# Causal attention and a gated FFN in one kernel: stores held back, two batches' DMA transposes split, and the order of the first three tiles placed anew

## The chip, the cores and the metric

One core of a Trainium2 chip. The metric is the time of one execution on the device, in microseconds (us). Each kernel is run several times, in rounds with the kernel before on the same chip. Differences below 2%: the class is "same".

## The reference

```python
q, k, v: (8, 8, 576, 64) float32            # batch, heads, sequence, head dim
w_gate, w_val: (512, 1536);  w_out: (1536, 512)

scores = q @ k.T / sqrt(64)
scores = where(block(i) >= block(j), scores, -1e9)   # blocks of 64 positions
attn   = softmax(scores) @ v
x      = attn.transpose(0, 2, 1, 3).reshape(4608, 512)
out    = (relu(x @ w_gate) * (x @ w_val)) @ w_out    # (4608, 512) float32
```

## The kernel before

The FFN works on nine tiles: tile j (0 to 7) is the first 512 positions of batch j, and the ninth is the last 64 positions (the "tail") of all eight batches. Attention of batch j + 1 is put between the FFN products of tile j. A table `AT` gives each piece of attention, load, cast or store a position, counted in FFN products (144 a tile), and a loop gives the pieces out in that order:

```python
for n in sorted(acts, key=lambda n: AT[n]):
    ffn(int(AT[n]) - place[0])                 # FFN products up to that position
    place[0] = max(place[0], int(AT[n]))
    acts[n]()                                  # then the piece itself
```

A position is only a place in the order of each engine's instructions. An engine that has nothing to wait for runs ahead of it.

The names in the table that this document needs:

```python
"q24":  # GpSimd casts q and k of batch 2, heads 4 to 7, from float32 staging to bf16 (2 x 128x1024);
        # SyncE transposes each by DMA into "perm" once it is cast
"v2":   # GpSimd casts v of batch 2 (2 x 128x1024)
"td0", "td1", "td2":  # VectorE casts half of the tail keys and of tail v of batch 0, 1, 2 (64x256 each)
"u0".."u3":  # copies from "perm" to qTm and kTm: q and k of batch 2, head pairs 0 to 3, by the engines
             # (q's, k's) named in HOW
"s8".."s15": # scores of round r = 4 * batch + head pair;  "x8".."x15": its output transposed to xT
"S0".."B2":  # the tails of batches 0 to 2; "A" and "B" are their two products with v
"d3":   # batch 3's q and k transposed by DMA: 2 main parts, 2 tails
```

Of the tiles that the traces name, xT is x transposed, the FFN's input; hT is relu(gate) times value, which VectorE writes for the FFN's second product; attnT is the exponential of the scores; qTm, kTm, qTt and kTt are q and k transposed, "mains" (the first 512 positions) and tails.

Batch 3's transposes go to SyncE's queue together, the tile's stores leave as each is done (those of tile 0 alone are held), and a tail's transpose follows at once on the tail's last product:

```python
def dma_transposes(b):
    m, tl = bfs[b, 0], bfs[b, 1]
    for t in range(2):
        nc.sync.dma_start_transpose(
            (qTm, kTm)[t][b % 2].rearrange("p c h n -> p (c h) n"), m[t])
    tails_by_dma(b, tl)                      # qTt, then kTt
...
# in the FFN, for each output group of tile j:
ob = sb.tile([128, 512], FP, name="ob", bufs=4)[:, 0 : n1 - n0]
nc.vector.tensor_copy(ob, op)
if store:
    store.pop()()
(store if j else late).append(lambda j=j: put(j, s, ob, n0, n1))   # put: DMA from ScalarE
...
# in a tail's piece:
def end():
    tail_av(b, 1, x)
    tail_to_xT(b, x)
```

(The code is cut.)

The softmax here doesn't subtract the row's maximum and nothing guards it: scores larger than these inputs give would overflow.

## Time and profile before

| | |
|---|---|
| median of 3 runs | 363.15 us (362.9 to 364.13) |
| the execution that was profiled | 365.12 us, span of the trace 363.3 |
| TensorE busy | 353.3 us of 363.3 (97%) |
| VectorE, ScalarE, GpSimd busy | 47%, 46%, 31% |
| TensorE idle 0 to 23, 95 to 116, end | 4.54, 1.81, 3.59 us |

A page of the profile lists each engine's busy time; the table of stretches gives it for chosen pieces of the span; the timeline shows single instructions with, in brackets, the idle time ahead of them and what ended it. A matmul's listed length runs past the start of the next, so waits of TensorE are counted here as start-to-start distance above what the same matmul takes when nothing is waited for (0.216 us for 512 columns, as the prediction works out). The execution in the trace took 2 us more than the median. The lines themselves are in the prediction below.

### The profile page before, as it was taken

How to read it: one execution, taken by the hardware profiler on the slowest of the kernel's cores; microseconds unless marked ns; L12 is line 12 of the kernel's file. 1: busy time of each engine (PE TensorE's matmuls, PEld its weight loads, DVE VectorE, ACT ScalarE, POOL GpSimd, SP SyncE). 2: the span in 40 equal slices, each digit the busy share in tenths (PEclk: the TensorE clock that was granted, in tenths of full speed). 3: DMA queues.
4: the chain of work that ended last, by engine and by line, in shares of the span. 5: the costliest groups of instructions: out<-in, count | busy, mean ns of one | idle time of the engine just before them, and what ended most of it. 6: DMA issues, size and time to landing. Idle time of an engine off the chain costs nothing.

```text
span 363.3 us, 7423 instructions
## 1 busy us (share of the span) xinstructions
PE 353.3 (97%) x2933; PEld 176.9 (49%) x2933; DVE 170.7 (47%) x426; ACT 167.9 (46%) x265; POOL 112.8 (31%) x157
## 2 busy tenths in 40 slices
PE   7899999999998999999999999999999999999996
PEld 3544455545544555555555454554455544444443
DVE  4663456677433363444445443554255434333432
ACT  4933676696325850666055625553365403302310
POOL 4647645695209500680049001930000000000000
PEclk9999999999999999999999999999999999999999
DMA  8999999999999995899449951997220130031013
GB/s 245 298 357 374 314 239 255 189 156 138 186 203 108 141 154 137 56 146 186 109 49 145 169 133 46 130 157 152 81 16 14 54 102 0 0 88 29 1 41 105
DMA packets 152083, 49.97 MB, mean 138 GB/s; under 512 B 134512, under 2 KB 145008, under 8 KB 152048
## 3 DMA queue, kind: packets, MB, share of 16 engines
q0 software_dynamic: 70480, 8.85, 46.7%
q1 hardware_dynamic: 76480, 31.86, 44.8%
q10 hardware_dynamic: 5088, 8.78, 7.2%
q8 instruction: 23, 0.38, 0.5%
q14 instruction: 12, 0.10, 0.1%
HBM read 37.75 MB, written 9.44 MB: 130 GB/s over the span
## 4 chain that ended last, share of the span: by engine, by line
PE 89%; DMA 5%; ACT 4%; DVE 1%; issue 0%; POOL 0%; SPq 0%; POOLq 0%; DVEq 0%
PE ffnp L663 49%; PE ffnp L748 23%; PE sc L450 3%; PE ffnp L585 2%; PE one L450 2%; DMA xT<-xnat 2%; DMA stage<-in_moe_w_gate_dram 2%; PE one L585 2%; ACT attnT L414 2%; PE one L663 1%; ACT attnT L455 1%; PE ffnp L547 1%; PE one L794 1%; DMA kTt<-k_bt 1%; PE ffnp L599 1%; PE one L599 1%
## 5 line engine op out<-in xcount | busy, mean ns | idle before, releaser
L679 DVE TENSOR_TENSOR hT<-gate_sb,ffnp 128x512 bf16<-128x512 bf16 x106 | 72.6, 685 | 96.5 <-PE ffnp L663 70.7
L673 ACT ACTIVATE gate_sb<-ffnp 128x512 bf16<-128x512 f32 x103 | 62.1, 605 | 103.3 <-PE ffnp L663 93.6
L663 PE MATMUL ffnp<-xT,wv 128*128 128x512 bf16 x376 | 100.7, 379 | 0.0
L663 PE MATMUL ffnp<-xT,wg 128*128 128x512 bf16 x364 | 99.0, 379 | 1.1 <-DMA xT<-xnat 0.4
L748 PE MATMUL ffnp<-wo,hT 128*128 128x512 bf16 (+2 forms) x444 | 98.8, 373 | 0.0
L748 PEld LDWEIGHTS <-hT 128*128 128x128 bf16 x444 | 41.8, 98 | 45.5 <-issue 0.6
L663 PEld LDWEIGHTS <-wv 128*128 128x128 bf16 x432 | 40.1, 98 | 45.5 <-issue 3.2
L663 PEld LDWEIGHTS <-wg 128*128 128x128 bf16 x432 | 39.8, 98 | 44.6 <-issue 3.6
L455 ACT ACTIVATE attnT<-sc 128x1024 bf16<-128x1024 f32 x56 | 56.8, 1044 | 0.0
L758 DVE COPY ob<-ffnp 128x512 f32<-128x512 f32 (+2 forms) x37 | 25.0, 676 | 45.1 <-PE ffnp L748 44.7
L338 POOL DMA_DIRECT2D q_bf<-in_q_dram x20 | 17.8, 903 | 76.3 <-DVE hT L679 52.0
L462 ACT ACTIVATE attnT<-one 128x512 bf16<-128x512 f32 (+1 forms) x28 | 15.0, 536 | 53.8 <-PE ffnp L450 53.8
L585 PEld LDWEIGHTS <-attnT 128*128 128x128 bf16 x640 | 26.5, 97 | 13.9 <-DVE attnT L803 1.3
L338 POOL DMA_DIRECT2D v_bf<-in_v_dram x30 | 24.3, 853 | 6.8 <-PE one L585 2.2
L450 PEld LDWEIGHTS <-kTm 64*128 64x128 bf16 x384 | 11.3, 94 | 15.6 <-issue 7.8
L338 POOL DMA_DIRECT2D k_bf<-in_k_dram x20 | 17.7, 933 | 0.0
L450 PE MATMUL sc<-qTm,kTm 64*128 64x512 bf16 (+1 forms) x168 | 16.9, 305 | 0.0
L585 PE MATMUL ffnp<-v_bf,attnT 128*128 128x65 bf16 x320 | 15.0, 194 | 0.0
L462 ACT ACTIVATE attnT<-ffnp 128x512 bf16<-128x512 f32 (+1 forms) x28 | 15.0, 534 | 0.0
L803 DVE MEMSET attnT<- 64x128 uint32 x59 | 9.0, 165 | 12.0 <-ACT attnT L455 10.2
L524 DVE TENSOR_TENSOR xnat<-ffnp,recip 128x256 bf16<-128x256 f32 x32 | 13.6, 424 | 1.1
L585 PE MATMUL one<-v_bf,attnT 128*128 128x65 bf16 x250 | 11.6, 193 | 0.7 <-POOL v_bf L220 0.7
(122 smaller groups left out, 293.8 us busy)
## 6 DMA issues: line engine op xcount, KB each, us to landing
out_dram<-ob ACTq DMA_DIRECT2D x29, 256.0 KB, 2.4
stage<-in_moe_w_val_dram SPq DMA_DIRECT2D x6, 512.0 KB, 8.2
stage<-in_moe_w_gate_dram SPq DMA_DIRECT2D x6, 512.0 KB, 8.7
stage<-in_moe_w_out_dram SPq DMA_DIRECT2D x6, 512.0 KB, 10.5
q_bf<-in_q_dram POOLq DMA_DIRECT2D x20, 128.0 KB, 4.3
k_bf<-in_k_dram POOLq DMA_DIRECT2D x20, 128.0 KB, 5.8
v_bf<-in_v_dram POOLq DMA_DIRECT2D x20, 128.0 KB, 6.1
stage<-in_v_dram SPq DMA_DIRECT2D x19, 128.0 KB, 5.4
```

Of the source, the lines that this page charges most:

```text
L338: ins = nc.gpsimd.dma_start(dst, part_of)
L450: nc.tensor.matmul(o, kTm[b % 2][head_of(hh), c, hp, :], qT, start=True, stop=True)
L455: return lambda: nc.scalar.activation(at[:, :, lo : lo + 512], sc, AF.Exp, scale=scale)
L462: nc.scalar.activation(at[:, hh, 1024 : 1024 + w], third[hh][:, 0:w], AF.Exp, scale=scale)
L524: nc.vector.tensor_tensor(out=out, in0=av[:, 0:m, 0:64], in1=recip[:, 0:m].to_broadcast([rows, m, 64]), op=AX.mult,)
L585: nc.tensor.matmul(av[:, p, :], at[:, col : col + 128], v_bf[b % 2][:, c, h, :], start=(p == 0), stop=(c == p), skip_group_check=True,)
L663: nc.tensor.matmul(to, (wg, wv)[t][f // 4][:, c, 128 * (f % 4) : 128 * (f % 4) + 128], x[:, c], start=(c == 0), stop=(c == 3),)
L673: nc.scalar.activation(gate_sb, gate, AF.Relu)
L679: nc.vector.tensor_tensor(out=h, in0=gate_sb, in1=val, op=AX.mult)
L748: nc.tensor.matmul(op, hT[f][:, 128 * s : 128 * (s + 1)], wo[f // 4][:, f % 4, n0:n1], start=(f == 0), stop=(f == 11),)
L758: nc.vector.tensor_copy(ob, op)
L803: nc.vector.memset(o, 0.0)
```

## The change

Its intent: take DMA work (tile 1's stores, the tails' transposes) out of the stretch around 95 to 116 us, where TensorE waits for DMA transposes; split batch 3's and batch 4's transposes into parts, and put batch 3's in another order and place; and place the order of everything in tiles 0 to 2 anew. The functional part:

```diff
-    def dma_transposes(b):
+    def dma_transposes(b, which=(0, 1, 2)):
         m, tl = bfs[b, 0], bfs[b, 1]
-        for t in range(2):
+        for t in which:
+            if t == 2:
+                tails_by_dma(b, tl)
+                continue
             nc.sync.dma_start_transpose(...)
-        tails_by_dma(b, tl)
...
-                xtails[b] = sb.tile([64, 512], BF, name="xtail", bufs=2)
+                xtails[b] = sb.tile([64, 512], BF, name="xtail", bufs=4)
...
-                (store if j else late).append(lambda j=j: put(j, s, ob, n0, n1))
+                (store if j > 1 else late).append(lambda j=j: put(j, s, ob, n0, n1))
...
             def end():
                 tail_av(b, 1, x)
-                tail_to_xT(b, x)
...
+                f"X{b}": lambda: tail_to_xT(b, x),
```

The table of positions has nearly 200 changed lines. Sorted by place (the start, positions below 140, is cut; its lines swap loads and casts of weights):

```diff
-            "td1": 164.5,
+            "td1": 155.98,
             "td0": 156.81,
...
-            "A0": 174.52,        # products with v of batch 0's tail
-            "B0": 178.89,
+            "A0": 180.62,
+            "B0": 184.99,
...
-            "u1": 190.06,
-            "u0": 190.06,
-            "v2": 191.07,
-            "q24": 191.07,
+            "q24": 190.06,
+            "u0": 190.39,
+            "u1": 190.39,
...
-            "u2": 207.72,
+            "v2": 203.58,
+            "u2": 203.99,
-            "s9": 208.6,
+            "s9": 206.14,
...
-            "d3": 260.7,
+            "d30": 263.9,        # q mains
+            "d32": 263.9,        # both tails
+            "d31": 263.91,       # k mains
-            "s12": 312.27,
+            "s12": 318.08,
...
+            "o4": 325.51,        # tile 1's stores
+            "X1": 330,           # tail of batch 1 to x
+            "X0": 332,
+            "o5": 339.19,
+            "o6": 352.67,
+            "X2": 355.13,
+            "o7": 366.92,
...
-            "u0": ("pool", "pool"),      # HOW: engines of the copies of q and k
-            "u1": ("dve", "dve"),
+            "u0": ("pool", "dve"),
+            "u1": ("pool", "dve"),
             "u2": ("dve", "dve"),
-            "r8": ("dve", "one", "ffn", None),
+            "r8": ("dve", "one", "ffn", ("dve", "sc")),   # x of round 8 over TensorE, not DMA
```

## The prediction

> **What bounds the kernel now.** I read the page's busy shares first, then the table of stretches, then the timeline of the one stretch in which TensorE is not full, and last the chain of waits. The first two lines are from the page, the rest is the table of stretches (busy us and instructions of each engine, granted clock, DMA share, GB/s).
>
> ```profile
> PE 353.3 (97%) x2933; PEld 176.9 (49%) x2933; DVE 170.7 (47%) x426; ACT 167.9 (46%) x265; POOL 112.8 (31%) x157
> ...
> DMA  8999999999999995899449951997220130031013
> ...
> 0.00:10.00 10.00, 7.26 (x42) 3.14 (x42) 4.50 (x14) 5.35 (x7) 5.01 (x21) 1.00 0.89 251
> 10.00:23.00 13.00, 11.20 (x147) 6.72 (x145) 9.05 (x27) 8.99 (x15) 6.89 (x13) 1.00 1.15 316
> 23.00:60.00 37.00, 37.00 (x291) 18.92 (x290) 18.03 (x42) 21.70 (x38) 22.56 (x27) 1.00 1.08 307
> 60.00:95.00 35.00, 34.90 (x395) 18.45 (x394) 23.99 (x63) 22.49 (x36) 22.86 (x29) 1.00 1.55 174
> 95.00:116.00 21.00, 19.19 (x170) 9.17 (x168) 7.17 (x16) 8.50 (x13) 6.31 (x8) 1.00 1.49 164
> 116.00:200.00 84.00, 84.00 (x774) 42.83 (x774) 40.33 (x113) 41.60 (x66) 34.81 (x45) 1.00 1.46 125
> 200.00:297.00 97.00, 97.00 (x827) 48.62 (x824) 44.70 (x120) 44.90 (x70) 14.35 (x18) 1.00 0.82 97
> 297.00:363.30 66.30, 62.71 (x303) 29.09 (x301) 22.89 (x34) 14.33 (x24) 0.00 (x0) 1.00 0.13 38
> ```
>
> TensorE sets the time. Of 363.3 us it is idle 10.05: 2.74 in the first 10 us, 1.80 up to 23 us, 0.10 from 60 to 95, 1.81 from 95 to 116, and 3.59 after its last matmul (eviction and store). From 116 to 297 it is not idle at all. No edit of this change can speed up those 181 us or the end, so all it can win lies in the 1.81 us in the middle and some of the 4.54 us of the start. The middle in the timeline, TensorE and the queue of SyncE:
>
> ```profile
> 97.34 5.46 SPq L347 DMA_TRANSPOSE qTm<-q_bf  x1
> ...
> 98.35 0.34 ACTq L647 DMA_DIRECT2D out_dram<-ob  x1
> ...
> 101.91 0.59 PE L663 MATMUL ffnp<-xT,wg 128*128 128x512 bf16 x2
> ...
> 102.77 0.38 PE L663 MATMUL ffnp<-xT,wg 128*128 128x512 bf16 x1 [0.26 <-DMA xT<-xnat]
> ...
> 103.03 3.81 SPq L347 DMA_TRANSPOSE kTm<-k_bf  x1
> 103.31 0.38 PE L663 MATMUL ffnp<-xT,wg 128*128 128x512 bf16 x1 [0.16 <-DMA xT<-xnat]
> ...
> 106.95 1.18 SPq L116 DMA_TRANSPOSE qTt<-q_bt  x1
> ...
> 107.58 1.03 PE L663 MATMUL ffnp<-xT,wv 128*128 128x512 bf16 x4
> ...
> 108.24 1.21 SPq L117 DMA_TRANSPOSE kTt<-k_bt  x1
> ...
> 109.00 0.28 PE L450 MATMUL one<-qTm,kTm 64*128 64x256 bf16 x1 [0.40 <-DMA kTm<-k_bf]
> ...
> 109.97 0.82 PE L663 MATMUL ffnp<-xT,wg 128*128 128x512 bf16 x3
> ...
> 111.76 0.29 PE L472 MATMUL one<-qTt,kTt 128*128 128x64 bf16 x4 [0.96 <-DMA kTt<-k_bt]
> ```
>
> Three waits, all for DMA transposes: tile 2's x (third and fourth product), batch 3's keys (its first scores), batch 3's tail keys. The chain of waits (start, length) goes through the same transposes:
>
> ```profile
> 95.97 7.30 DMA xT<-xnat
> ...
> 108.24 3.47 DMA kTt<-k_bt
> ...
> 328.60 20.72 PE ffnp L663 x96
> ```
>
> The last line is the rate: 20.72 / 96 = 0.2158 us a product. With it the waits have their true size, start to start: 102.77 - (101.91 + 2 x 0.216) = 0.43; 103.31 - 102.77 - 0.216 = 0.32; 109.00 - (107.58 + 4 x 0.216) = 0.56; 111.76 - (109.97 + 3 x 0.216) = 1.14. Sum 2.45 us, more than the 1.81 of idle time, since a matmul's shown length runs past the start of the next.
>
> **What the Trainium skill says.** "TensorE: Matmul & The Clock Gate", Step-by-step: what each phase is for, gives about 216 ns between 512-column products back to back; the trace has 215.8. "Perfetto Trace Analysis", Identifying the Most-Contended Engine, says that matmul busy time misjudges the distance to the roofline; the same product is listed at 379 ns, so I count starts. "DMA: Bandwidth & Descriptors", Issuing engines are not separate DMA queues, says that transfers of all issuers run on the same 16 engines and interleave. It agrees: the x transpose issued at 95.97, among GpSimd's loads and ScalarE's stores, took 7.30 us to land, where the tile's median is 3.9. "Perfetto Trace Analysis", DMA Instruction — HWDGE (DVE, Sync), says that the issuing instruction ends with the generation of descriptors, before the data has moved: keys took 3.81 us to issue and were still waited for at 109.00, 5.97 after the issue began.
>
> **The change, part by part.** Positions in the table of the schedule count FFN products, 144 a tile; tile 2 begins at 288, which TensorE reaches at 101.91.
>
> 1. Stores of tile 1. Their positions are 325 to 367 instead of right after each eviction. The stores at 98.35 and (in the timeline too) 93.97 and 102.81 leave the busy stretch. A store holds 256 KB, so 0.77 MB; at the 164 GB/s of this stretch that is 4.7 us of transfer, at the 316 of the start 2.4. There are four output buffers, and tile 2 needs the first again near 396, after all four stores: no wait. Nothing on TensorE.
>
> 2. Tails' transposes to x. Those of batches 0, 1 and 2 go to 332, 330 and 355. One (batch 1, formerly at 83.74) leaves the stretch before tile 2; 1.2 us of SyncE's queue. Four buffers instead of two make this legal. Read only in the last tile (328 us): no wait.
>
> 3. Round 8's x goes over TensorE instead of DMA: 4 transposes of 128 columns, about 4 x 0.056, and a change between chains of near 0.1: +0.33 us of TensorE. One DMA transpose less (1.2 us of issue); its DVE copy of 0.42 lies beside.
>
> 4. Batch 3's transposes. Equal positions keep the listing's order, so the order is: q mains, both tails, k mains. The tail keys' wait (1.14) should vanish. But the last x transpose comes later: its round's second product with v moves from 259.11 to 263.76, and the tail's scores of batch 2 (0.76 with their changes of array shape) now go ahead of it. Counting TensorE: 94.27 for round 10's second half, +0.31, +0.22, +0.76, +0.22, +0.31, +0.43 gives 96.5; DVE adds 1.15 as before, so x is issued near 97.65, not 95.97. Then q mains from 99.0 for 3.2 to 5.5 us (4.3), tails 2 x 1.24, k mains from 106.0. Landing takes 4.3 at the least, median 5.9: 110.3 to 111.9. If both issues are fast, 109.1.
>
> 5. Batch 3's scores move from 312.27 to 318.08 (+5.8 x 0.216 = 1.25). Without waits TensorE is there at 101.91 + 0.33 + 30 x 0.216 + 0.6 for a tail product = 109.3. So the wait for keys is not 0.56 but between 0 and 2.6; I take 1.3. The x waits (0.75) should go: 97.65 plus about 4 lands before 102.9, where the fourth product wants it.
>
> Middle: -2.45 - 0.15 (the scores' first pair, which lost time as well: 109.01 to 109.31 in the timeline for 256 columns that take 0.11) + 0.33 + 1.3 = about -1.0 us.
>
> 6. Start. The order of the q and v loads stays; the first gate and value weights swap, so gate weights land about 1.5 us earlier. In the timeline, though, TensorE's last wait of the start is for x of head pair 2, whose copy on ScalarE (20.33) stood behind the cast of the second gate weights, which waited 2.42 us for their load. That load keeps its place behind the same bytes. And a cast of value weights (about 0.6) is now put on ScalarE between the two: the copy may come at 20.9. Against that, pair 3's transposes now stand ahead of those products. I count +0.2, between -0.6 and +0.7.
>
> 7. Rounds 12 to 15 take other PSUM banks, tails of batch 2 and batch 4's q and k transposes other places. From 116 on there is no TensorE idle time to win; I count 0, at worst +0.5.
>
> Sum: -1.0 + 0.2 + 0 = -0.8: 363.15 - 0.8 = about 362.3. Because the new placing looks searched for, and my figures for queues are the pessimistic end, I say 362.2.
>
> **Rivals.** (a) Everything works: no wait at keys, none at x, 0.5 gained at the start: -2.6 + 0.33 - 0.5, about 360.4. For it: issue times of 2.8 for k mains occur when DMA is quiet. (b) The wait only changes its name: k mains are now last in SyncE's queue and wait 2.6 or more, perhaps slowed by batch 4's loads, which begin at 109.7 before; then the middle gains nothing, and with the start's +0.2 to +0.7 the time is 363.5 to 364. For it: the queue is in order, and q mains and tails before keys take 6.8 us of it. (c) The stretch is bound by GpSimd's small loads, not by stores: they hold 46.7% of the engines' time in the page's list of queues against 7.2% for stores. Then x still lands late, 0.5 us of wait stays, and 362.8 results. I think (a) 25%, (b) 30%, the rest between.
>
> **Range and chances.** Repeats of before spread from 362.9 to 364.13. From (a) and (b) I take 360.6 to 364.0. 2% is 7.3 us; the idle time within reach is at most 6.4, and a loss of 7 would need several new waits of the largest size seen. Faster 1%, same 98%, slower 1%.
>
> **What would show it.** Right: 116 to 297 stays full; no TensorE wait for kTt; the x waits are gone or under 0.3; the one wait left in the middle is for kTm at batch 3's first scores, 0.5 to 2.5 us; no store is issued between 90 and 110. Wrong: a wait for xT over 0.5 us; a new TensorE wait after 116; TensorE's start of dense work off from 22 us by more than 0.7; or kTm issued before 104 and not waited for, which would make it 360.5.

## The result, and the profile after

| | before | after |
|---|---|---|
| median | 363.02 us (4 runs, 362.79 to 364.13) | 364.08 us (4 runs, 363.84 to 364.63) |
| profiled execution, its span | 365.12 us, 363.3 | 364.63 us, 362.8 |

Ratio 1.0025, 95% interval 1.0001 to 1.0049: class same, and by about 1 us slower. A ratio here is the mean time of one kernel's fast runs over that of the other's of the same rounds, so it is not quite the ratio of the medians.

The table of stretches of the changed kernel (columns as in the prediction: stretch, length, then busy us and instructions of PE, PEld, DVE, ACT, POOL, the granted clock, DMA share, GB/s):

```profile
10.00:23.00 13.00, 10.87 (x145) 6.80 (x146) 9.41 (x29) 9.11 (x14) 5.19 (x11) 1.00 1.15 316
60.00:95.00 35.00, 33.31 (x360) 17.61 (x358) 24.55 (x56) 21.96 (x36) 24.38 (x29) 1.00 1.49 167
95.00:116.00 21.00, 21.00 (x216) 11.10 (x215) 9.62 (x24) 8.79 (x15) 5.06 (x7) 1.00 1.10 118
116.00:200.00 84.00, 84.00 (x775) 42.74 (x774) 39.78 (x111) 41.86 (x66) 36.55 (x49) 1.00 1.44 137
```

The middle, 95 to 116, is full: 21.00 of 21 instead of 19.19. Of the 1.81 us that were idle there, 1.59 have come back as idle time from 60 to 95: 33.31 busy instead of 34.90. The start lost 0.3 more than before (10.87 instead of 11.20).

The middle in the timeline, SyncE's queue and the first scores of batch 3:

```profile
101.22 1.96 SPq L350 DMA_TRANSPOSE qTm<-q_bf  x1
103.28 1.58 SPq L116 DMA_TRANSPOSE qTt<-q_bt  x1
104.96 1.21 SPq L117 DMA_TRANSPOSE kTt<-k_bt  x1
106.35 1.32 SPq L350 DMA_TRANSPOSE kTm<-k_bf  x1
...
111.22 0.28 PE L452 MATMUL one<-qTm,kTm 64*128 64x256 bf16 x1
```

The order is the one predicted: q mains, tails, k mains. The keys, issued at 106.35, landed at 110.62; TensorE asked for them at 111.22, so nothing waits. But TensorE is there 1.9 us later than the 109.3 that the prediction worked out. It lost most of them from 62 to 66 us:

```profile
61.87 1.04 POOL L195 CAST q_bf<-stage 128x1024 bf16<-128x1024 f32 x1 [0.87 <-DMA stage<-in_q_dram]
62.01 1.04 DVE L207 CAST k_bt<-stage 64x256 bf16<-64x256 f32 x1
...
63.22 1.05 POOL L195 CAST k_bf<-stage 128x1024 bf16<-128x1024 f32 x1 [0.32 <-DMA stage<-in_k_dram]
63.40 1.02 DVE L207 CAST k_bt<-stage 64x256 bf16<-64x256 f32 x1
...
64.56 0.38 PE L296 MATMUL ffnp<-ident,k_bt 128*128 128x128 bf16 x4 [0.64 <-DVE k_bt L207]
64.77 0.69 DVE L681 TENSOR_TENSOR hT<-gate_sb,ffnp 128x512 bf16<-128x512 bf16 x1
```

The same VectorE instructions in the kernel before:

```profile
61.58 0.29 DVE L207 CAST k_bt<-stage 64x256 bf16<-64x256 f32 x1
...
62.84 0.69 DVE L679 TENSOR_TENSOR hT<-gate_sb,ffnp 128x512 bf16<-128x512 bf16 x1 [0.65 <-PE sc L663]
...
64.51 0.29 DVE L207 CAST k_bt<-stage 64x256 bf16<-64x256 f32 x1
```

A 64x256 cast took 0.29 us and now takes 1.04 and 1.02, both times beside a GpSimd cast of 1.04 or 1.05 that began 0.14 to 0.18 us ahead of it and ended about 0.15 us before it. In the order of the change, GpSimd's casts (`q24`) come ahead of the copies `u0` and `u1`, and VectorE's tail casts of batch 1 (`td1`) directly ahead of those of batch 0 (`td0`); so two pairs of casts meet. VectorE takes its instructions in order: the product hT comes at 64.77 instead of 62.84, and TensorE waits 0.80 us at 63.73 for the tail keys and 0.77 at 65.31 for the bank (a piece of the memory that TensorE writes to) that hT frees. Further on it waits 0.61 at 76.34, also for hT, and 0.29 at 50.02, for a VectorE memset of attnT.

In the chain of waits the two products hT (64.77, 1.30 us) now stand, and the DMA transposes that stood there before (7.30 for xT and 3.47 for kTt) are gone.

### The profile page after: what moved, and what is told of

Read it like the earlier page. It is cut to its first block, busy times and chain, and to the rows that moved or that the text cites. A ratio compares the mean times of both kernels' runs of the same rounds, so it can differ in the third digit from the quotient of the medians.

```text
span 362.8 us, 7419 instructions
## 1 busy us (share of the span) xinstructions
PE 352.5 (97%) x2937; PEld 177.7 (49%) x2937; DVE 173.8 (48%) x426; ACT 167.6 (46%) x265; POOL 114.9 (32%) x158
## 4 chain that ended last, share of the span: by engine, by line
PE 91%; DMA 3%; DVE 2%; ACT 1%; POOL 1%; issue 1%; SPq 0%; DVEq 0%; POOLq 0%
PE ffnp L665 49%; PE ffnp L750 26%; PE sc L452 3%; PE ffnp L587 2%; PE one L452 2%; PE one L587 2%; DMA stage<-in_moe_w_gate_dram 2%; DMA stage<-in_k_dram 1%; PE one L665 1%; PE ffnp L549 1%; PE ffnp L601 1%; DVE hT L681 1%; PE one L601 1%; ACT attnT L416 1%; PE sc L587 1%
## 5 line engine op out<-in xcount | busy, mean ns | idle before, releaser
L338 POOL DMA_DIRECT2D k_bf<-in_k_dram x20 | 18.5, 960 | 0.0
L587 PE MATMUL ffnp<-v_bf,attnT 128*128 128x65 bf16 x300 | 14.0, 194 | 0.2
L526 DVE TENSOR_TENSOR xnat<-ffnp,recip 128x256 bf16<-128x256 f32 x30 | 12.7, 425 | 1.0
L665 PE MATMUL ffnp<-xTt,wg 128*128 128x512 bf16 x48 | 12.3, 379 | 0.0
```

The source lines that it names most:

```text
L338: ins = nc.gpsimd.dma_start(dst, part_of)
L526: nc.vector.tensor_tensor(out=out, in0=av[:, 0:m, 0:64], in1=recip[:, 0:m].to_broadcast([rows, m, 64]), op=AX.mult,)
L587: nc.tensor.matmul(av[:, p, :], at[:, col : col + 128], v_bf[b % 2][:, c, h, :], start=(p == 0), stop=(c == p), skip_group_check=True,)
L665: nc.tensor.matmul(to, (wg, wv)[t][f // 4][:, c, 128 * (f % 4) : 128 * (f % 4) + 128], x[:, c], start=(c == 0), stop=(c == 3),)
```

## The experiments

Twelve kernels in three groups of four; each group ran on one chip, five rounds, with the kernel before beside it. Before's own runs were in group 1: 364.85, 362.92, 362.81, 362.77, 362.58, 364.11, 362.43, 362.54, 367.11, 363.11, 362.66; in group 2: 362.4, 362.25, 362.53, 364.62, 364.77, 362.3, 362.64, 364.67, 362.59, 362.28, 362.83; in group 3: 363.27, 365.32, 362.55, 362.63, 362.43, 362.65, 364.22, 362.48, 364.93, 362.34, 364.84. So the kernel before has two levels, 362.25 to 363.27 (23 runs) and 364.11 to 367.11 (10 runs), with nothing between them, although none is 1.5% above the fastest and so none counts as slow. The granted clock does not tell them apart: 0.993 to 1.000 in the lower, 0.995 to 1.000 in the upper. Keep this in mind with every interval below: they are about ±0.4% wide, mostly because of this.

| kernel | median us | runs over 364 | ratio to before, 95% interval |
|---|---|---|---|
| before, again (1) | 364.53 | 4 of 6 | 1.0028 [0.9985, 1.0071] |
| after, again (1) | 365.23 | 6 of 6 | 1.0047 [1.0010, 1.0084] |
| early part old, late part new (1) | 363.16 | 0 of 6 | 0.9998 [0.9962, 1.0035] |
| early part new, late part old (1) | 364.57 | 6 of 6 | 1.0039 [1.0002, 1.0076] |
| after, GpSimd casts behind the copies (2) | 363.25 | 1 of 6 | 1.0009 [0.9980, 1.0038] |
| before, GpSimd casts ahead (2) | 362.67 | 0 of 6 | 0.9988 [0.9958, 1.0018] |
| before, tile 1's stores held (2) | 363.90 | 3 of 6 | 1.0015 [0.9983, 1.0047] |
| early old, late new, tail transposes behind (2) | 367.58 | 6 of 6 | 1.0123 [1.0088, 1.0158] |
| after, casts behind and copies' engines as before (3) | 363.69 | 3 of 6 | 1.0009 [0.9975, 1.0042] |
| early old, late new, stores at once (3) | 364.07 | 4 of 6 | 1.0023 [0.9988, 1.0058] |
| early old, late new, keys ahead of tails (3) | 362.66 | 0 of 6 | 0.9982 [0.9951, 1.0013] |
| after, one tail cast back (3) | 364.08 | 4 of 6 | 1.0013 [0.9981, 1.0045] |

My theory going in: the early part of the new order costs 1.5 to 2 us through the casts that meet, and the late part wins back what the middle had lost. The rivals: the late part itself costs (held stores come back as collisions later), or the gain in the middle was never there in an ordinary execution.

### 1. Both kernels again

No edit.

> The kernel before, unchanged, for a second trace of it. Both theories: ratio 1.000. The theory that the middle waits vary from run to run (the profiled run of before took 365.12 us, its timed runs 363.0): this trace has less than the 2.45 us of waits for the x, key and tail-key transposes between 95 and 116 us, near 0.5 to 1. The rival that the profile is typical: again 2.2 to 2.7 us there.

> The changed kernel, unchanged, for a second trace. Both theories: ratio 1.002 to 1.004 to before, 364.1 us; the waits at 63.7, 65.3 and 76.3 us (0.80, 0.77, 0.61 us start to start) come again within 0.2, since they come from the order of casts on VectorE and GpSimd and not from DMA; no TensorE wait between 95 and 116 us.

The second trace of the kernel before fell on an execution of 362.65 us (span 360.8):

```profile
60.00:95.00 35.00, 34.90 (x395) 18.45 (x394) 24.03 (x63) 22.50 (x36) 22.67 (x29) 1.00 1.61 182
95.00:116.00 21.00, 21.00 (x195) 10.60 (x192) 9.25 (x22) 8.99 (x14) 7.03 (x9) 1.00 1.35 157
```

There is no idle time in the middle (0.5 to 1 us of waits was expected). The three waits of 2.45 us that the whole prediction was about belong to the execution of 365.12 us, and 363.3 - 360.8 = 2.5 us is just their size. What differed is the DMA. Two stretches of 1 us of the trace before (first fence), and the first of them in the trace of the ordinary execution (second fence); the last column is GB/s:

```profile
86.00:87.00 1.00, 1.00 (x15) 0.57 (x14) 0.54 (x4) 1.00 (x2) 1.00 (x2) 1.00 1.86 24
87.00:88.00 1.00, 1.00 (x15) 0.64 (x14) 1.00 (x3) 0.28 (x1) 0.77 (x1) 1.00 0.26 21
```

```profile
86.00:87.00 1.00, 1.00 (x15) 0.54 (x14) 0.53 (x4) 1.00 (x2) 1.00 (x2) 1.00 1.27 92
```

In the execution of 365.12 us, 28 packets, nearly all of 128 or 256 bytes and each over 0.9 us long, were under way from 85.40 for 2.56 us, while a DMA transpose of x began (85.92) amid GpSimd's loads; in the ordinary one nine, from 85.13 for 1.46 us. After it, GpSimd's first load of v landed at 97.28 instead of 93.17, the last x at 103.27 instead of 101.47, kTm at 108.96 instead of 107.01 and kTt at 111.71 instead of 108.76. Such standstills (six or more packets of at most 512 bytes, each over 0.9 us long, overlapping) of 1 to 3 us are in every trace, six to eleven each; whether the upper level of the times is always such a longer standstill I can't show, since only one trace fell on each level.

The changed kernel had, again, 0.77 at 65.52, 0.61 at 76.54 and 0.29 at 50.92, and a new wait of 0.75 at 145.09 for tile 3's x. The wait of 0.80 for the tail keys did not come again, a miss of this expectation: GpSimd's first cast came later in this execution (63.76 instead of 61.87), both of VectorE's key casts took 0.29, and the cast that met it was the one of tail v behind them (1.07 us from 63.87), so that only hT was late. Which casts meet, and whether the loss is 1.57 or 0.77 us, varies between executions.

### 2. Which half of the new order costs

Edit: all positions under 200 and their engines of one kernel, the rest of the other.

> Positions and engines of all that lay before 200 as in the kernel before, the rest (held stores, held tail transposes, split batch-3 transposes, round 8 over TensorE) as changed. Theory 1, the early part loses 2 to 2.5 us and the late part gains 1 to 1.5: 361.6 us, ratio 0.996. Theory 2, the late part gains the whole 2.5 us of the profile and the early loses 3.5: 360.6. Theory 3, the late part is what costs and the early is harmless: 364 us.

> The reverse: the changed kernel's places and engines before 200, the kernel before from there on, stores of tile 1 and tail transposes at once. Theory 1: 365.2 us, ratio 1.006, with the waits of 63.7, 65.3 and 76.3 us and those of the middle both there. Theory 2: 366.5. Theory 3: 363.

Early new, late old has the changed kernel's waits again (0.92 at 63.70, 0.77 at 65.40, 0.61 at 76.43, 0.30 at 49.98) and 1.19 in the middle, and all its runs are at 364.25 or above. Early old, late new has none of them and stays between 362.48 and 363.94. So the loss is in the early part. The gain that the theory gave the late part did not come: early old, late new was to take 361.6 us, 0.996 of before, and takes 363.16, 0.9998. What is left in the middle of early old, late new is one wait for keys, 0.64 start to start:

```profile
103.33 1.32 SPq L350 DMA_TRANSPOSE kTm<-k_bf  x1
...
109.08 0.28 PE L452 MATMUL one<-qTm,kTm 64*128 64x256 bf16 x1 [0.48 <-DMA kTm<-k_bf]
```

This is the wait that the prediction put at 1.3, and which the changed kernel hides by coming late. The issue took 1.32 us, but the keys landed 5.70 after its start. The Trainium skill ("Perfetto Trace Analysis", DMA Instruction — HWDGE (DVE, Sync)) says that the profiler shows the issue without the movement of the data; the trace agrees.

### 3. Is it the casts?

```diff
 # after, GpSimd casts behind the copies
-            "q24": 190.06,
+            "q24": 190.5,
```

> The changed kernel with one position moved: GpSimd's casts of batch 2's second half (q24) from 190.06 to 190.5, behind the unpermuting copies, as the kernel before has them. Theory of the shared port (VectorE's tail casts wait for GpSimd's casts beside them: 1.04 and 1.02 us instead of 0.29): the casts take 0.29 again, TensorE's waits at 63.7 and 65.3 us (0.80 and 0.77 start to start) go, the one at 76.3 stays; 1.3 us less than the changed kernel, ratio to before 1.001. Rival, VectorE's queue (batch 1's tail cast was moved ahead, from 164.50 to 155.98, and fills VectorE at the wrong moment): casts 0.29, but at least 0.5 us of those waits stays.

VectorE's two key casts took 0.29 again (62.04 and 62.68), both waits near 64 and 65 us are gone, and the ratio is 1.0009 where the changed kernel's own had been 1.0025 and 1.0047 (the intervals overlap; the trace is the evidence). The wait of 0.6 near 75 stays. The Trainium skill ("SBUF — State Buffer", Who interferes with whom) says that VectorE and GpSimd share one pair of ports to SBUF, that VectorE's copies and casts can use it, and that "Whoever issues first gets the shared pair for the whole instruction"; the other waits until it is over. The changed kernel's trace agrees: 0.29 became 1.04 beside a 1.04 cast issued 0.14 earlier.

```diff
 # before, GpSimd casts ahead
-            "q24": 191.07,
+            "q24": 190.0,
```

> The kernel before with that one part alone: q24 from 191.07 to 190.0, ahead of the unpermuting copies. Shared port: GpSimd casts near 62 to 64.5 us, at least one of VectorE's casts of k tails takes about 1.0 us, TensorE gets a wait of 0.3 to 0.9 us between 63 and 66 us; ratio 1.001 to 1.003. Rival (queue order): casts 0.29, no new wait, ratio 1.000.

A miss. The casts met here too, but on another instruction:

```profile
61.88 1.12 DVE L214 CAST v_bf<-stage 64x256 bf16<-64x256 f32 x1
...
61.82 1.04 POOL L195 CAST q_bf<-stage 128x1024 bf16<-128x1024 f32 x1 [0.94 <-DMA stage<-in_q_dram]
```

One cast was blocked, hT slid from 62.84 to 63.03 only, TensorE lost 0.2 us, and the time didn't move. In the kernel before, `td1` stands behind hT (64.51), so GpSimd's second cast met nothing. It takes both moves:

```diff
 # after, one tail cast back
-            "td1": 155.98,
+            "td1": 164.4,
```

> The changed kernel with only the cast of batch 1's tail keys back at position 164.4 (before: 164.5); GpSimd's casts of head pair 2 stay ahead of the unpermutes, as in the change. Theory (the loss near 63 to 65 us needs both moves: the two engines' casts must fall on the same microsecond AND stand ahead of what TensorE needs next): at most one of VectorE's two key tail casts takes 1 us, TensorE's two waits of 0.8 near 63.7 and 65.3 shrink to a sum of at most 0.8, ratio to before 1.001 to 1.003. Rival (GpSimd's early casts alone do it): both waits stay, sum 1.4 or more, ratio 1.003 to 1.005.

With GpSimd's casts still ahead, but `td1` back, VectorE's one remaining key cast took 0.44 (at 62.81), and both waits are gone (no wait over 0.23 between 58 and 70). Either move without the other costs at most 0.2 us here; both together cost 1.57 us in one trace of the changed kernel and 0.77 in the other. The ratio, 1.0013, is in the range that the theory gave; its interval contains 1 and can't tell the kernels apart, the trace can.

### 4. The wait near 76 us

```diff
 # after, casts behind and copies' engines as before
+            "q24": 190.5,
-            "u0": ("pool", "dve"),
-            "u1": ("pool", "dve"),
+            "u0": ("pool", "pool"),
+            "u1": ("dve", "dve"),
```

> The changed kernel with two things as before: GpSimd's casts of head pair 2 behind round-5 unpermutes (this alone gave 1.0009 of before), and the engines of unpermutes 0 and 1 as before, so that VectorE has no key halves to copy near 74 us. Theory (shared lock of VectorE and GpSimd): the TensorE wait of 0.6 near 75 to 76 us goes as well, TensorE is busy 34.7 or more of the 35 us from 60 to 95, and the time falls by about 0.5 against that of the kernel with only the casts moved, to 0.999 to 1.000 of before. Rival (the wait comes from the order of the FFN's rounds, not from the copies): the wait stays within 0.2 us of what it was, 1.001 of before.

A miss: the wait of 0.61 is still there. The edit did not take the copies off VectorE: with the engines of before, `u1` gives it q and k of head pair 1, where the change gave it k of head pairs 0 and 1, two copies either way. The timeline of this kernel:

```profile
72.85 2.48 POOL L228 CAST v_bf<-stage 128x1024 bf16<-128x1024 f32 x2 [1.57 <-PE ffnp L549]
...
74.34 1.44 DVE L253 COPY kTm<-perm 128x512 bf16<-128x512 bf16 x1
...
75.81 0.69 DVE L681 TENSOR_TENSOR hT<-gate_sb,ffnp 128x512 bf16<-128x512 bf16 x1
...
76.55 0.27 PE L452 MATMUL ffnp<-qTm,kTm 64*128 64x256 bf16 x1 [0.44 <-DVE hT L681]
```

The copy beside GpSimd's second cast of v took 1.44; the one right ahead of it (73.81) took 0.60. hT stands behind the copy, and the scores of batch 2's head pair 0 wait for the bank that hT frees. What the change made late here is the cast of v. `v_bf` has two buffers, so batch 2's v goes where batch 0's was, and its cast waits for the products with v of batch 0's tail, which the change moved from 174.52 and 178.89 to 180.62 and 184.99 (`A0`, `B0`): the last of them started at 72.68 and the cast at 72.85, in the changed kernel at 73.19 and 73.36. In the kernel before the last one started at 69.52 and the first cast at 70.10, and the same pair of copies, 1.02 and 1.01 us beside the second cast, left hT done in time. Early old, late new, with `A0` and `B0` in their old places, has no such wait, but differs in much else; putting them back alone was not tried. So this step is argued from the traces.

### 5. What the late part does: stores, tails, order

```diff
 # before, tile 1's stores held (positions 325.51, 339.19, 352.67, 366.92)
-                (store if j else late).append(...)
+                (store if j > 1 else late).append(...)
```

> The kernel before with tile 1's stores alone held to 325.51 to 366.92. If stores in the stretch made the waits between 95 and 116 us of the first profile: no run above 363.5 us, none of those waits in the trace, median as before's fast executions (362.6). Rival (DMA engines stand still for 1 to 2.5 us when a transpose starts beside GpSimd's loads, stores or not): one run in four still above 364, standstills over 1 us still in the trace between 80 and 103 us.

Holding the stores alone did not narrow the spread (362.15 to 364.82), the standstills stayed (85.09 for 1.47 us, 98.41 for 1.52), and a new wait of 0.76 for tile 3's x came at 142.78. The place to which the stores were moved isn't idle: batch 4's q transpose, issued at 119.00, took 13.5 us to land there (11.1 in both traces of the kernel before). A wait of 0.50 to 0.76 for tile 3's x, between 142 and 146 us, is in four of the nine traces of kernels that hold tile 1's stores and in none of the five that do not; that fits the held stores as its cause but does not show it.

```diff
 # early old, late new, tail transposes behind
-            "X1": 330,
-            "X0": 332,
+            "X1": 351.2,
+            "X0": 351.4,
```

> Early part of the kernel before, late part of the changed one, and the tails' transposes of batches 0 and 1 put behind round 12's in SyncE's queue (351), so that they are really held: at 330 they were issued at 104.7 us, right behind batch 3's keys. If they slow the keys (5.7 us to land there): keys land in about 4.3 us, the wait of 0.64 us at 108.2 goes, median 362.3, ratio 0.998. Rival (keys are late because they are last in the queue): the wait stays over 0.4 us and the ratio is 1.000.

In the change, the tails' transposes sit at 330 and 332 by the table, but SyncE has nothing to wait for and issues them right behind the keys (104.70 and 106.73 in early old, late new). Put behind x12 they did leave: keys landed in 4.55 us and their wait is gone, as expected. The time rose by about 4.5 us all the same (1.0123 against 0.9998 of before):

```profile
124.93 0.34 ACTq L649 DMA_DIRECT2D out_dram<-ob  x1
125.37 0.60 ACT L675 ACTIVATE gate_sb<-ffnp 128x512 bf16<-128x512 f32 x1 [4.12 <-DMA xT<-xnat]
```

ScalarE issues the stores and also evicts the gates. Its store at 124.93 did not start until the transpose of x12, issued at 117.56, had landed at 124.91; the evictions behind it in ScalarE's order stood still, and TensorE with them for 3.7 us. The instruction records of the two traces say why it is this transpose. The store waits on the DMA semaphore 105. With this edit, x12's transpose is the last DMA ahead of it that signals 105 too; without it, that is an earlier store of the same tile (issued at 112.08), long done, and x12's transpose signals 108. So in this program DMAs share a few semaphores, a later one waits for an earlier one on the same, and moving two transposes in the table changed who shares with whom.

```diff
 # early old, late new, stores at once: the four positions o4 to o7 removed
-                (store if j > 1 else late).append(...)
+                (store if j else late).append(...)
```

> Early part of before, late part of the change, but tile 1's four stores go out at once, as before. Theory (what the late part does for the middle is in the order and places of batch 3's transposes; the stores have nothing to do with it): runs between 362.4 and 364, ratio to before 0.998 to 1.001, and a middle with at most a wait for keys of about 0.6 us, no wait for tile 2's x over 0.3. Rival (held stores are what took the spread and the waits away): the waits for x come back at 0.3 to 0.8 us and part of the runs lie at 364 to 365; ratio 1.002 to 1.004.

Mixed. No wait for x came back, which the rival wanted, but the wait for keys grew to 1.12 (issued 104.56, landed 5.91 later) and the runs lie from 363.77 to 365.18. The time fits the rival, the waits do not: with three stores issued between 95 and 102, this trace has q mains landing 4.92 after issue instead of 4.42 in the next kernel, and everything behind them in SyncE's queue late. Within the new late part, holding the stores seems worth about a microsecond; the intervals overlap.

```diff
 # early old, late new, keys ahead of tails
-            "d32": 263.9,
-            "d31": 263.91,
+            "d31": 263.90,
+            "d32": 263.91,
```

> Early part of before, late part of the change, but batch 3's key mains are issued ahead of its tails, as before. The prediction's step 4 says that the tails ahead of the mains take the tail keys' wait away at the price of 2 x 1.24 us of later key mains. If that is right: kTm lands about 2.5 us earlier, so its wait (0.6) goes, and the tail keys land after 110.5, with a wait of 0.3 to 1.2 us for them instead. Sum between -0.3 and +0.6 us. Rival (with the scores at position 318 instead of 312 both have time enough, and the order of the tails is worth nothing): neither wait shows over 0.3, and the time is 0.3 to 0.6 below that of the kernel with the change's order.

The rival of this expectation was right: both waits vanish.

```profile
101.07 2.43 SPq L350 DMA_TRANSPOSE kTm<-k_bf  x1
...
109.29 0.28 PE L452 MATMUL one<-qTm,kTm 64*128 64x256 bf16 x1
```

The keys landed at 105.63 and the tail keys at 107.41, both before TensorE wants them (109.29 and 111.75): with the scores moved to 318 there is time for both, and the order of the tails is worth nothing. All six runs are within 362.37 to 363.36. By its ratio this is the best version: old order up to position 200, new one behind it, keys first. It is not free of waits: its trace has 0.69 us for tile 3's x at 142.97. Its median, 362.66, equals that of the kernel before in its rounds (362.65), and the ratio, 0.9982, can't be told from 1. None of its runs is at the upper level; together with early old, late new that is 0 of 12 runs, against 10 of 33 of before in the three groups (14 of 39 with the repeat). That the late part does this is not shown: "before, GpSimd casts ahead", which keeps the old late part, has 0 of 6 as well. Against the changed kernel it was not run on one chip; by the ratios to before, 0.9982 against 1.0025 and 1.0047, it is 1.5 to 2.4 us faster, with intervals that just touch.

## Why the prediction was right or wrong

It said 362.2, and the changed kernel takes 364.08: at the upper edge of the range of 360.6 to 364.0 and just past it. The class was right. The sign of the change was wrong: -0.8 predicted, +1.06 measured.

- **What bounds the kernel.** Right that it is TensorE, and that only the start and the middle have idle time to win. Wrong in a premise: the 2.45 us of waits were read from an execution of 365.12 us and then taken off a median of 363.15, of runs that for the most part did not have them. "-1.0 us" for the middle was a gain over the profiled execution only. (One reading in it is off by little: 109.01 to 109.31 less 0.11 is 0.19, not 0.15.) Over an ordinary one it is 0 at best, as the repeat of before shows (21.00 of 21 busy).
- **Step 1, stores.** Right that no TensorE work hangs on them in the middle: none is issued between 90 and 111 (114.22, 115.95, 121.20, 125.53). Their new place is not free, though: held stores alone gave a 0.76 us wait at 142.78, and the changed kernel's second trace has 0.75 at 145.09, one of the prediction's own signs of being wrong (a new wait after 116).
- **Step 2, tails.** Right that nothing waits for them. But they don't move to where the table puts them: SyncE issued two of them at 107.71 and 109.74, right behind the keys.
- **Step 3, x8 over TensorE.** +0.33 predicted; the four transposes took 0.22 (90.27 to 90.49).
- **Step 4, order.** Issue order as worked out. x was issued at 99.82, not 97.65, with TensorE 2.1 us late by then (tile 2 began at 104.05, not 101.91); k mains at 106.35 (106.0 predicted), landed 110.62 (110.3 to 111.9 predicted). That these agree is luck: x was 2.2 us later than worked out, and the issue of q mains (1.96, not 4.3) 2.3 us shorter. That the tails had to go ahead to save their 1.14 us was wrong: keys ahead of tails has neither wait.
- **Step 5, wait for keys.** 1.3 predicted, 0 found in the changed kernel, because TensorE came at 111.22 instead of 109.3. Without the early loss it is 0.64, with stores at once 1.12: inside the 0 to 2.6 that was worked out, and below the 1.3 that was taken.
- **Step 6, start.** Mechanism as predicted: the value weights' cast went between on ScalarE and the copy of x came at 20.86 (20.9 predicted). The size varies. The first output product of tile 0 starts, over six traces with the new early part, at 42.13 to 42.20 (three) or 42.96 to 43.12 (three), and over eight with the old at 41.54 to 42.23; the means are 42.61 and 41.96, so +0.65 on average where +0.2 was predicted. Why it has two levels is open; the first loads landed about 0.2 us later in the slow start that I looked at. No experiment put the start back alone.
- **Step 7, the rest.** This is the step that failed. "From 116 on there is no TensorE idle time to win; I count 0, at worst +0.5": it looked for what could be won, and the stretch from 23 to 95, full before, was not looked at for what could be lost. There the new order lost 0.29 + 0.80 + 0.77 + 0.61 us less the 0.24 that before has there, 2.2 us. The 0.80 and 0.77 are casts of two engines that meet (shown in experiment 3), the 0.61 a copy that meets a cast (argued from traces); the cause of the 0.29 stays open. The diff shows both moves, `q24` ahead of `u0` and `td1` next to `td0`, and the trace of before shows VectorE and GpSimd casts close by.
- **The sum.** -0.8 put on the profiled execution's own 365.12 would have been 364.3, near the 364.63 of the profiled execution after. That is luck: the middle came out about 1.4 better than -1.0 (-2.45 - 0.15 + 0.22 = -2.4), and the stretch before it 2.2 worse. **The rivals**: (b), 363.5 to 364, had the right time for the wrong reason, since no wait for keys is in it; of (a) the middle came true (no wait for keys or x), its 0.5 us at the start and its time did not; (c)'s 0.5 of x waits didn't come.

## What to carry to other kernels

Before taking a wait off a median, see whether the profiled execution ran at the median: here it was 2 us slower, and its waits were about those 2 us. When an order is placed anew, go through the full stretches too, for what can be lost: pairs of casts and copies of VectorE and GpSimd that come to lie side by side ahead of something that TensorE needs. And a place in a table of order is no time: an engine with nothing to wait for issues at once, and a DMA issue in a computing engine's order can hold that engine.

## What the Trainium skill lacked or had wrong

- "SBUF — State Buffer" (Who interferes with whom) agreed with the traces wherever casts met. It names ratios of slowing without the sizes of the two instructions; here a 64x256 float32-to-bf16 cast went from 0.29 to between 1.02 and 1.15 us beside a 128x1024 cast of 1.04, and a 128x512 bf16 copy from 0.60 to 1.44.
- No page that I found has the DMA standstills of 1 to 3 us, six to eleven in each trace, many at times when DMA transposes run among GpSimd's loads ("DMA: Bandwidth & Descriptors" would be the place). In one trace 2.56 us of it and about 2 us of execution time went together.
- No page that I found says that a kernel can have two levels of time: here 362.25 to 363.27 and 364.11 to 367.11, 23 and 10 runs.
- No page that I found warns of the time that it costs when a store issued by ScalarE waits for the landing of another DMA, which uses the same semaphore, and holds the evictions behind it ("DMA: Bandwidth & Descriptors" would be the place): 4.12 us of ScalarE idle and 3.7 us of TensorE here.
